# The state's read of x in 32-column weights, four heads in four column groups of the PE array, with its sums from ScalarE's accumulator

## Chip, cores and metric

One core of a Trainium2 chip. The metric is the device time of one execution in microseconds (us), the median of several runs. All runs quoted are fast: the granted TensorE clock was 0.998 to 1.000 of full speed in every one of them. Ratios are the mean time of one kernel's fast runs over that of the other's fast runs of the same rounds, so they are not quite the ratio of the medians quoted beside them.

## The reference

Eight batches, each with 8 heads, 512 tokens of 64 dimensions and 32 states. The tokens read the state, the state reads the tokens, and both results go through a two-dimensional Fourier mix, a norm and an MLP. The part at issue is `sread`.

```python
scores2 = scale * np.matmul(state, x.transpose(0, 1, 3, 2))
scores2 = scores2 - scores2.max(-1, keepdims=True)
a2 = np.exp(scores2)
a2 /= a2.sum(-1, keepdims=True) + 1e-09
sread = np.matmul(a2, x)                       # per head: (32 x 512) @ (512 x 64)
...                                            # Fourier mix, norm
ch = np.maximum(un @ w_ch1, 0.0) @ w_ch2       # the MLP, most of the work
return (u + ch).astype(np.float32)
```

## The kernel before

Two words first. Each matmul leaves two records in the trace: the load of its weight (LDWEIGHTS, engine PEld) and the matmul (engine PE), for which the columns of the other operand, the moving columns, are streamed. PSUM is the memory that the results land in.

`E` holds exp(scores) with tokens on the partitions: four blocks `si` of 128 tokens, two halves `g` of four heads, and 128 columns (4 heads x 32 states). `turn_scores` turns it over into `ET`, with states on the partitions. The state's read uses `E` as the weight. A weight has the columns of four heads, so each matmul multiplies every one of the four heads' states with every one of the four heads' x, and only the four blocks on the diagonal are used. A column of ones beside x gives the sums.

```python
def turn_scores(g):
    p = qt("eTp")
    for si, o, rhs in (...):                                     # cut
        nc.tensor.matmul(p[:, o:o + rhs.shape[1]], lhsT=E[:, si, g, :], rhs=rhs, start=True, stop=True)
    nc.scalar.copy(ET[:, g, :], p)

def sread():
    rcs = wk.tile([128, 2], F32, name="rcs", tag="rcs")
    for g in range(2):
        p = qt("srp")                                            # one of three PSUM tiles
        for si in range(4):
            nc.tensor.matmul(p[:, 0:257], lhsT=E[:, si, g, :], rhs=xin[:, si, 257 * g:257 * g + 257],
                             start=(si == 0), stop=(si == 3))
        nc.vector.reciprocal(rcs[:, g:g + 1], p[:, 256 * g:256 * g + 1])
        for hh in range(4):
            ...                                                  # cut: c0, ph of the head
            o = XR[0:32, 0, c0:c0 - 64:-1]
            i = p[ph, 1 - g + 64 * hh:65 - g + 64 * hh]
            if g == 0 and b > 0:
                nc.vector.tensor_scalar(o, in0=i, scalar1=rcs[ph, g:g + 1], scalar2=None, op0=ALU.mult)
            else:
                nc.scalar.activation(o, i, AF.Copy, scale=rcs[ph, g:g + 1])

second = [
    lambda: xread(256, True, "xrp", XR[:, 0, 1:513]),
    sread,
    None,
    lambda: xread(0, False, "xfp", XF[:, 0, 0:512], apart=(b == 0)),
    low if b > 1 else lambda: (low(), fold_early()),             # 32 low rows: two matmuls of 260 columns
    ...
]
```

These steps are woven between the matmuls of the MLP (`ph`, layer 1, and `po`, layer 2), so that TensorE always has something to do.

The softmax here doesn't subtract the row's maximum and nothing guards it: scores larger than these inputs give would overflow.

## Time and profile before

| | before |
|---|---|
| median (range) | 320.87 us (320.67 to 321.31) |
| span of the profiled run | 319.8 us |
| busy: TensorE, VectorE, ScalarE | 304.9, 189.1, 145.8 us |
| state's reads from batch 2 on | 6 x 8 matmuls of 257 columns, 0.885 us of TensorE's stream each |

A TensorE record lasts longer than the matmul holds the stream (a 512-column one is recorded at 379 ns and they follow each other every 216), so the cost of a group of matmuls is read from starts: the start of the next group less its own. The 216 ns for 512 columns and 110 for 257 are 0.416 ns a column, or 2.4 columns a nanosecond, and some 3 ns for each matmul. The prediction below shows the lines.

### The profile page before, as it was taken

The page shows a single profiled execution, that of the slowest core. Times are in us where ns is not written, and L with a number is a line of the kernel's source. Part 1 is how long each engine was busy: PE and PEld are TensorE (multiplying, and loading weights), DVE is VectorE, ACT ScalarE, POOL GpSimd, SP SyncE. Part 2 cuts the span into 40 slices and gives each one's busy share as a digit, 9 for nine tenths or more (in the row PEclk, how much of TensorE's full clock was granted, in tenths as well). Part 3 has the DMA queues.
Part 4 walks back from the last instruction along what each step waited for, and adds up shares of the span by engine and source line. Part 5 has one row for each costly group of instructions (what it writes and reads, how often), then busy time and mean ns, then how long its engine had stood idle before and what let it go on. Part 6 is the DMA issues. An engine that isn't in the chain of part 4 may idle for free.

```text
span 319.8 us, 5768 instructions
## 1 busy us (share of the span) xinstructions
PE 304.9 (95%) x2206; PEld 177.8 (56%) x2206; DVE 189.1 (59%) x451; ACT 145.8 (46%) x283; POOL 73.1 (23%) x167
## 2 busy tenths in 40 slices
PE   5979998899999999999999999999999999999995
PEld 5858986454554555555645554555454544455444
DVE  8797576669586693781816865595658583101112
ACT  6798763844544444334343434434443332343200
POOL 8658693500240020300320024001200030000000
PEclk9999999999999999999999999999999999999999
DMA  7998997425855925239243443630352025302064
GB/s 141 203 197 162 207 188 132 80 65 118 177 87 117 197 68 124 64 82 194 69 96 66 84 116 82 133 84 33 81 86 66 33 47 120 82 35 66 35 137 126
DMA packets 111532, 34.22 MB, mean 107 GB/s; under 512 B 102928, under 2 KB 107280, under 8 KB 111504
## 3 DMA queue, kind: packets, MB, share of 16 engines
q1 hardware_dynamic: 100784, 28.08, 41.8%
q0 software_dynamic: 4224, 4.19, 8.1%
q10 hardware_dynamic: 6496, 1.57, 2.4%
q8 instruction: 17, 0.28, 0.4%
q14 instruction: 11, 0.09, 0.1%
HBM read 22.43 MB, written 14.02 MB: 114 GB/s over the span
## 4 chain that ended last, share of the span: by engine, by line
PE 79%; DVE 14%; ACT 3%; issue 2%; POOL 1%; DMA 1%; DVEq 0%; POOLq 0%; ACTq 0%
PE po L719 31%; PE ph L653 29%; PE gp L533 3%; PE warm L739 2%; PE ph L663 2%; PE srp L429 2%; DVE U L503 2%; DVE st L314 1%; PE yp L499 1%; DVE XR L419 1%; DVE ot L684 1%; PE yp L498 1%; PE xrp L410 1%; DVE XQ L466 1%; PE xfp L410 1%
## 5 line engine op out<-in xcount | busy, mean ns | idle before, releaser
L719 PE MATMUL po<-w,hT 128*128 128x512 bf16 x496 | 125.0, 379 | 0.0
L653 PE MATMUL ph<-unT,w 128*128 128x512 bf16 x448 | 114.5, 379 | 0.9 <-DVE ot L684 0.8
L655 ACT ACTIVATE hT<-ph 128x512 bf16<-128x512 f32 x112 | 66.8, 597 | 102.2 <-PE ph L653 102.0
L653 PEld LDWEIGHTS <-w 128*128 128x128 bf16 x576 | 51.3, 98 | 48.9 <-issue 1.7
L719 PEld LDWEIGHTS <-hT 128*128 128x128 bf16 x496 | 47.5, 98 | 44.9
L684 DVE SCALAR_TENSOR_TENSOR ot<-po,rstd,U 128x512 f32<-128x512 f32 (+1 forms) x33 | 24.2, 733 | 55.8 <-PE po L719 51.5
L543 POOL COPY GL<-G 128x128 bf16<-128x128 bf16 x8 | 2.4, 299 | 120.6 <-ACT G L541 120.6
L503 DVE TENSOR_TENSOR U<-yp,XR 128x512 f32<-128x512 f32 x16 | 10.9, 683 | 22.4 <-PE yp L499 22.4
L314 DVE BATCH_NORM_STATS2 st<-U 128x6 f32<-128x512 f32 x32 | 21.8, 681 | 0.1
L319 POOL TENSOR_TENSOR rstd<-rstd,mhalf 128x1 f32<-128x1 f32 x34 | 20.3, 596 | 2.7
L440 ACT ACTIVATE XR<-srp,rcs 32x64 bf16<-32x64 f32 x36 | 11.1, 309 | 21.0 <-DVE rcs L431 20.4
L318 POOL TENSOR_TENSOR rstd<-mv,epst 128x1 f32<-128x1 f32 x34 | 6.5, 191 | 60.5 <-DVE mv L316 60.5
L739 PE MATMUL warm<-ident 128*128 128x128 bf16 x182 | 15.4, 241 | 3.5 <-POOL ident masks.py:199 3.4
L541 ACT CAST G<-gp 128x288 bf16<-128x288 f32 x31 | 12.2, 396 | 12.7 <-PE gp L533 6.7
L663 PE MATMUL ph<-unT,w 128*128 128x128 bf16 x256 | 16.2, 219 | 0.2 <-ACT unT L577 0.2
L739 PEld LDWEIGHTS <-ident 128*128 128x128 bf16 x182 | 13.6, 110 | 4.2 <-POOL ident masks.py:199 3.4
L663 PEld LDWEIGHTS <-w 128*128 128x128 bf16 x256 | 15.2, 98 | 0.6 <-issue 0.3
L533 PEld LDWEIGHTS <-XQ 128*128 128x128 bf16 x96 | 8.6, 98 | 9.3 <-DVE XQ L466 3.8
L136 POOL CAST xin<-xs 128x2048 bf16<-128x2048 f32 x7 | 13.2, 1891 | 0.0
L567 DVE TENSOR_SCALAR ub<-U,mv 128x512 bf16<-128x512 f32 x24 | 12.3, 512 | 1.0 <-DVE mv L316 0.2
L410 PEld LDWEIGHTS <-ET 128*128 128x128 bf16 x80 | 7.2, 98 | 9.2 <-DVE XL L419 0.8
L419 DVE TENSOR_TENSOR XR<-xrp,rs 128x512 bf16<-128x512 f32 x16 | 11.1, 695 | 0.9 <-POOL XR L276 0.3
(181 smaller groups left out, 368.0 us busy)
## 6 DMA issues: line engine op xcount, KB each, us to landing
xs<-in_x_dram SPq DMA_DIRECT2D x30, 256.0 KB, 4.6
w<-in_moe_w_ch_dram POOLq DMA_DIRECT2D x8, 512.0 KB, 10.8
out_dram<-ot SPq DMA_DIRECT2D x15, 256.0 KB, 2.7
r_dram<-ot SPq DMA_DIRECT2D x14, 256.0 KB, 2.2
out_dram<-r_dram SPq DMA_DIRECT2D x14, 256.0 KB, 3.7
xs<-in_x_dram ACTq DMA_DIRECT2D x2, 256.0 KB, 3.5
l_dram<-ot SPq DMA_DIRECT2D x2, 256.0 KB
r_dram<-ot ACTq DMA_DIRECT2D x2, 256.0 KB
```

Of the source, the lines that this page charges most:

```text
L314: nc.vector.bn_stats(st6, u)
L319: nc.gpsimd.tensor_tensor(rstd, rstd, mhalf, op=ALU.pow)
L410: nc.tensor.matmul(ph[:, 0:260], lhsT=ET[:, g, c0:c0 + 128], rhs=rhs, start=True, stop=True)
L419: nc.vector.tensor_tensor(ov, in0=p[ps, :, 0:256].rearrange("p g (h d) -> p g h d", d=D), in1=rs[ps].unsqueeze(3).to_broadcast([n, 2, 4, D ...
L503: nc.vector.tensor_add(u.rearrange("p (k r) -> p k r", r=2), p.rearrange("p (r k) -> p k r", r=2)[:, 0:u.shape[1] // 2, :], x.rearrange("p ...
L533: nc.tensor.matmul(p[:, 0:NM], lhsT=XQ[:, j, c, :], rhs=tab[c], start=(c == 0), stop=(c == 2 and j != 2))
L653: nc.tensor.matmul(ph[:, o:o + n], lhsT=w1[:, c, f * 128:(f + 1) * 128], rhs=un_of[key][:, c, :], start=(c == 0), stop=(c == DC - 1))
L655: nc.scalar.activation(hT[:, per * i:per * i + per, :].rearrange("p a b -> p (a b)"), ph, AF.Relu, scale=-1.0 if key in flipped else 1.0)
L663: nc.tensor.matmul(ph[:, o:o + 128], lhsT=w1[:, c, f * 128:(f + 1) * 128], rhs=un_of[key][:, c, 128 * r:128 * r + 128], start=(c == 0), st ...
L684: nc.vector.scalar_tensor_tensor(ot[:, cols], in0=po_of[i][:, 0:cols.stop - cols.start], scalar=rstd, in1=u[:, cols], op0=ALU.mult, op1=AL ...
L719: nc.tensor.matmul(po_of[i], lhsT=h_of[key][:, f, i * 128:(i + 1) * 128], rhs=w2[:, f, :], start=(f == 0), stop=(f == FC - 1))
L739: nc.tensor.matmul(t[:, 0:128], lhsT=ident, rhs=ident, start=(i == 0), stop=(i == n - 1))
```

## The change

The intent is to stop computing what is thrown away. Each head gets its own 32-column weight and its own 64 columns of x, and writes its own 32 partitions of one PSUM tile. A weight of 32 columns that writes 32 partitions occupies one quarter of the array's columns (a column group), so that four heads may work side by side. The column of ones falls out of the matmul; the sums come instead from the copy that evacuates `ET`, as ScalarE adds up each row as it copies.

```diff
+        sums = wk.tile([128, 2], F32, name="sums", tag="sums")
...
-            nc.scalar.copy(ET[:, g, :], p)
+            nc.scalar.activation(ET[:, g, :], p, AF.Copy, accum_out=sums[:, g:g + 1])
...
+        def sread_by_head():
+            p = qt("srp")
+            for g in range(2):
+                for si in range(4):
+                    for hh in range(4):
+                        c0 = 1 + 256 * g + 64 * hh
+                        nc.tensor.matmul(p[32 * hh:32 * hh + 32, 64 * g:64 * g + 64], lhsT=E[:, si, g, 32 * hh:32 * hh + 32],
+                                         rhs=xin[:, si, c0:c0 + 64], start=(si == 0), stop=(si == 3))
+            rcs = wk.tile([128, 2], F32, name="rcs", tag="rcs")
+            nc.vector.reciprocal(rcs, sums)
+            o = XR[0:32, 0, 512:0:-1].rearrange("p (g h d) -> p h g d", g=2, d=D)
+            for hh in range(4):
+                ph = slice(32 * hh, 32 * hh + 32)
+                nc.vector.tensor_tensor(o[:, hh], in0=p[ph, 0:128].rearrange("p (g d) -> p g d", g=2),
+                                        in1=rcs[ph].unsqueeze(2).to_broadcast([32, 2, D]), op=ALU.mult)
...
-            sread,
+            sread if b < 2 else sread_by_head,
```

## The prediction

> **What bounds the kernel now.** I began with the busy shares and the chain of waits on the page.
>
> ```profile
> PE 304.9 (95%) x2206; PEld 177.8 (56%) x2206; DVE 189.1 (59%) x451; ACT 145.8 (46%) x283; POOL 73.1 (23%) x167
> ...
> PE 79%; DVE 14%; ACT 3%; issue 2%; POOL 1%; DMA 1%; DVEq 0%; POOLq 0%; ACTq 0%
> ```
>
> TensorE is busy for 95% of the 319.8 us span, and no other engine is above 59%. A busy matmul record counts its pipeline too, so I next read TensorE's timeline, where the start of the next group gives the cost in the stream. This is the stretch around the state's read of the last batch (L429):
>
> ```profile
> 234.27 0.38 PE L410 MATMUL xrp<-stb,ET 128*128 128x260 bf16 x2
> 234.49 1.03 PE L719 MATMUL po<-w,hT 128*128 128x512 bf16 x4
> 235.35 1.05 PE L429 MATMUL srp<-xin,E 128*128 128x257 bf16 x8
> 236.24 1.02 PE L719 MATMUL po<-w,hT 128*128 128x512 bf16 x4
> ```
>
> The starts touch: four 512-column matmuls fill 0.86 us (216 ns each), eight 257-column ones fill 236.24 - 235.35 = 0.89 us (110 ns each). The table of busy time by stretch says the same: TensorE 34.00 us busy of 34.00 in each of 108 to 142, 181 to 215 and 215 to 249 us. From 63 us, where batch 2 reads its state, until 260 us, the table of waits charges TensorE with 2.0 us in all: 0.7 for one transposition, 0.6 for the fold (VectorE, L466), 0.5 for an output and 0.2 for an activation. So in the part that the change touches a nanosecond on TensorE is a nanosecond of the end, and a nanosecond on VectorE or ScalarE is nearly free.
>
> **What the Trainium skill says.** Three places bear on it.
> - "TensorEngine Tiling (Array Packing)", Key Properties and Instruction Overhead: tiles of the array work independently, but "Changing tiling mode (not just tile) drains the TensorE", and a matmul of 1 column costs as much as one of 60. Its restrictions add that column tiling turns the fast weight load off. Every group in this trace is marked 128*128, so the trace shows neither the gain nor the drain.
> - "TensorE: Matmul & The Clock Gate", Part 3 (Measured speedup vs the span model): a pack of tiles takes one matmul's duration and about 4 ns for each further tile; three column tiles at 512 columns gave 2.38 times. That is for 512 columns, where ours have 64. Nothing here confirms it yet.
> - The same page, Part 2 (Back-to-back issue gap): N / 2.4 + 2.5 ns when warm. This gives 109.6 ns for 257 columns and 29.2 for 64. The trace agrees, with 110 above and with the scores' group, which has 64 columns and a new weight for each matmul:
>
> ```profile
> 116.77 0.40 PE L385 MATMUL esp<-sT,xT 128*128 128x64 bf16 x8
> 117.00 0.81 PE L719 MATMUL po<-w,hT 128*128 128x512 bf16 x3
> ```
>
> Eight pairs of weight load and matmul take 0.23 us, 29 ns a pair. I found no price for ScalarE's accumulator output on a page.
>
> **The change part by part.** Only batches 2 to 7 change, so each figure is times 6.
>
> *TensorE, removed:* per batch 8 matmuls of 257 columns, 0.885 us on the path (0.89, 0.88 and 0.88 in the timeline of three batches), 5.3 us in all. That is the ceiling of a gain by this route: 1.7%, even if the new read cost nothing.
>
> *TensorE, added:* per batch 32 pairs, each a 32-column weight and 64 moving columns. The array's useful work falls from 8 x 257 = 2056 column slots to a quarter of 32 x 64 = 2048, if four column groups run at once; if they run one after another it stays the same. The number of instructions goes up fourfold, since the order of the changed program on TensorE has 288 rows more (6 batches x 24 more loads and 24 more matmuls). At the 29 ns of the scores' pairs: 32 x 29 = 0.93 us, which is 0.05 more per batch, +0.3 us in all. I take this as the base, since a 64-column matmul is near the floor already (about 28 ns for 32 columns: the three matmuls of L397 that begin with the identity take 0.14 us, two of which are 128 columns at 56).
>
> *TensorE, the mode:* each read goes from whole-array tiles to column tiles and back, two switches. If the array drains, the cost is what lies between a matmul's streaming and its end. The scores' record lasts 193 ns with 27 ns of streaming (64 / 2.4), so about 166 ns. Two at full price are 0.33 us per batch, 2.0 in all. Part of it can lie beside weight loads already under way, so I count half, +1.0 us.
>
> *ScalarE:* the rows concerned, from the groups by form:
>
> ```profile
> L440 ACT ACTIVATE XR<-srp,rcs 32x64 bf16<-32x64 f32 x36 | 11.1, 309 | 21.0 <-DVE rcs L431 20.4
> L438 DVE TENSOR_SCALAR XR<-srp,rcs 32x64 bf16<-32x64 f32 x28 | 7.9, 281 | 0.6
> L398 ACT CAST ET<-eTp 128x512 bf16<-128x512 f32 x12 | 7.0, 584 | 1.6 <-PE eTp L397 1.5
> L431 DVE RECIPROCAL rcs<-srp 128x1 f32<-128x1 f32 x16 | 2.7, 166 | 3.2 <-PE srp L429 2.9
> ```
>
> Removed are 4 x 309 = 1.24 us per batch, 7.4 us in all, and the wait for the second reciprocal that held ScalarE's queue (20.4 us at 8 places, 2.5 or so each). Added is the sum of each of the 12 casts of L398. If it is read by a separate small instruction of some 200 ns (my guess), that is 0.4 us per batch. ScalarE gets about 5 us lighter, all beside TensorE. On the path it can give back only the single 0.2 us that TensorE waited for an activation.
>
> *VectorE:* removed are 2 x 166 + 4 x 281 = 1456 ns; added are one reciprocal (168) and four products of 32 x 128 read from PSUM. From the products of 256 columns (425 ns, L413) and of 512 (690, L419) the slope is 1.04 ns a column, so 128 columns take about 425 - 133 = 292 ns. Sum: 168 + 4 x 292 = 1336. So VectorE gets 0.1 us lighter per batch. In batch 2 TensorE waits 0.6 us for VectorE's fold, so about 0.1 of it may come back there.
>
> *Buffers:* one PSUM tile of the pool of three in place of two, and it is free as soon as VectorE's products end, not after ScalarE's four late copies (2.7 us after its last matmul's start in the last batch). TensorE shows no wait for that pool in the changed stretch, so this is worth nothing.
>
> Sum: +0.3 + 1.0 - 0.2 = **+1.1 us**, from 320.87 to about **321.9 us**.
>
> **The rivals.**
> - *The column groups overlap as the skill's span model has it.* Then eight rounds of four take 8 x (29 + 3 x 4) = 0.33 us per batch (estimate from that page), 0.56 less than now: -3.3 us; with half the drains -2.3, so about 318.5 us. For it speaks that consecutive matmuls go to different groups and all share one PSUM tile in different quadrants. Against it: each of the 32 matmuls has its own weight load in front, and the floor on a short matmul may be one of issue, which tiles do not lift. I give it 3 in 10.
> - *Loads and matmuls stop overlapping.* Without the fast weight load, or because a column tile's load must wait for the matmul before it, a pair may cost the load and the matmul in turn, 29 + 29 = 58 ns: 32 x 58 = 1.86 us, and with both drains 2.19, which is 1.3 per batch more than now: +7.8 us, about 328.7 us. For it speaks that the trace has no load narrower than the array, so the overlap seen on L385 is not proved for these. I give it 2 in 10, the full price less often.
> - *A wait elsewhere gives more than the sum.* If the ScalarE queue, blocked behind the second reciprocal for 2.6 us per batch, were holding up the relu tiles, freeing it would shorten the chain by several us. The timeline speaks against it: TensorE's starts touch right after each state read. I count it at zero.
>
> **Range and chances.** The three ways give 318.5, 321.9 and 328.7. The quick one sets the low end with some freedom, **317.6**; the slow one at about half its price sets the high end, **326.5**. A gain over 2% needs -6.4 us, more than the whole read costs now (5.3), so **0.02**. A loss over 2% needs +1.07 us per batch, thus a read of 1.95 us, 61 ns a pair with no drain or 51 with both: the slow rival at nearly its full price, **0.11**. The rest, **0.87**, is within 2%.
>
> **What would show it.** In the timeline of the changed kernel, the start of the group after the state's read less the read's start should be 0.93 to 1.26 us, in place of 0.885; 0.35 to 0.5 would mean that the groups overlap, and above 1.8 that loads and matmuls alternate. The start of the first 32-column matmul should lag by up to 0.17 us after the 216 ns slot of the matmul before it, and so should the first matmul after the read, if there is a drain. ScalarE's busy time should fall by about 5 us and its wait on L431 go, VectorE's by about 0.7 us, and TensorE should still show no wait for either from 78 to 260 us. The prediction is wrong if the read's slot is outside 0.5 to 1.8 us, or if the slot is as said and the end still moves by over 3 us, which would mean that a wait elsewhere, or the accumulator's cost, was on the path.

## The result

| | before | after |
|---|---|---|
| median, same chip (4 runs each) | 321.09 us | 318.71 us |
| ratio of the fast runs | | 0.9931, 95% interval 0.9914 to 0.9948 |
| span of the profiled run | 319.8 us | 317.1 us |
| busy: TensorE, VectorE, ScalarE | 304.9, 189.1, 145.8 us | 300.2, 188.1, 139.7 us |
| one state's read in TensorE's stream, batches 2 to 7 | 0.885 us | 0.453 us |

The class is "same" (within 2%), but the gain of 0.7% is clear of noise. Two later repeats of the changed kernel gave 0.9926 and 0.9909. Lines below carry the changed kernel's numbers, 18 higher for code behind the new function: L719 became L737 and L653 became L671.

The page's busy shares and chain of the changed kernel, the answer to the first fence of the prediction:

```profile
PE 300.2 (95%) x2317; PEld 174.7 (55%) x2350; DVE 188.1 (59%) x445; ACT 139.7 (44%) x271; POOL 73.1 (23%) x167
...
PE 79%; DVE 13%; ACT 2%; issue 2%; POOL 1%; DMA 1%; DVEq 0%; POOLq 0%; ACTq 0%
```

TensorE is as much the bound as before. It has some 2350 matmuls in place of 2206 (33 records are missing from the trace; the loads, complete at 2350, show it).

The state's read of batch 7 in the timeline of the changed kernel, loads included (start, duration, engine, line, what, and in brackets the idle time before it):

```profile
232.27 1.03 PE L737 MATMUL po<-w,hT 128*128 128x512 bf16 x4
...
233.23 0.30 PEld L450 LDWEIGHTS <-E 128*32 128x32 bf16 x32 [0.42 <-issue]
233.23 0.43 PE L450 MATMUL srp<-xin,E 128*32 128x64 bf16 x32
...
233.58 0.55 PEld L737 LDWEIGHTS <-hT 128*128 128x128 bf16 x4
...
233.81 0.81 PE L737 MATMUL po<-w,hT 128*128 128x512 bf16 x3 [0.16 <-issue]
```

The last group has lost a record: it has four loads from 233.58 on but only three matmuls. So the "idle 0.16" in front of it is not idle. The repeat of the changed kernel has the same place in batch 5 with every record:

```profile
167.10 1.03 PE L737 MATMUL po<-w,hT 128*128 128x512 bf16 x4
168.06 0.43 PE L450 MATMUL srp<-xin,E 128*32 128x64 bf16 x32
168.42 1.04 PE L737 MATMUL po<-w,hT 128*128 128x512 bf16 x4
```

The read has three parts. In front: 168.06 - 167.10 = 0.96 us, 0.09 more than the 0.86 of four 512-column matmuls. The matmuls: the record of 0.43 us less the 0.193 us that one of them lasts is 0.236 us from the first start to the last. Behind: 0.36 - 0.236 = 0.124 us from the last start to the next group. The sum is 0.453 us. The starts themselves, in ns from the read's first matmul (batch 4 of the changed kernel, taken from the trace's records), show what happened:

```
0 3 7 10 | 38 42 45 49 | 74 78 81 85 | 103 107 110 114 | 132 137 139 143 | 162 166 168 172 | 193 197 200 207 | 222 227 229 237
```

Four matmuls start within 10 to 15 ns, then nothing until the next four, 29 to 31 ns after the start of the ones before (38 and 36 for the first two rounds), which is about what 64 columns take to stream (29 ns). That is how four column groups at work at once would look; the run with one group, below, tests it.

The other engines, from the groups by form of the changed kernel (busy us, mean ns, idle before and its releaser):

```profile
L399 ACT ACTIVATE ET<-eTp 128x512 bf16<-128x512 f32 x12 | 7.1, 596 | 1.6 <-PE eTp L398 1.5
L457 DVE TENSOR_TENSOR XR<-srp,rcs 32x128 bf16<-32x128 f32 x24 | 6.9, 287 | 1.3 <-PE srp L450 0.8
L441 ACT ACTIVATE XR<-srp,rcs 32x64 bf16<-32x64 f32 x12 | 3.7, 309 | 2.4 <-DVE rcs L432 2.3
...
L399 ACT ACTIVATION_READ_ACCUMULATOR ET<-eTp 128x1 f32 x12 | 2.4, 202 | 0.0
...
L453 DVE RECIPROCAL rcs<-sums 128x2 f32<-128x2 f32 x6 | 0.9, 154 | 0.0
```

The accumulator is read by an instruction of its own, 202 ns. ScalarE's wait for the reciprocal fell from 20.4 us to 2.3 (what is left is batches 0 and 1). TensorE's waits of the changed kernel between 63 and 260 us:

```profile
PE tp L594 <- ACT ub L583: 0.7, 1, 0.7
PE po L737 <- issue: 0.6, 4, 0.2
PE gp L551 <- DVE XQ L484: 0.6, 1, 0.6
PE ph L671 <- DVE ot L702: 0.4, 1, 0.4
PE xfp L411 <- DVE XL L420: 0.2, 1, 0.2
```

The 0.6 of "issue" is the lost records again, four times 0.16. The rest is 1.9 us where it was 2.0: the 0.2 that the kernel before waited for an activation (L655) went, and 0.2 for VectorE (L420) came. So the sum is 6 x (0.885 - 0.453) = 2.6 us, and the spans differ by 2.7.

### The profile page after: what moved, and what is told of

Its sections match the earlier page's. It is cut to its first block, busy times and chain, and to the rows that moved or that the text cites. A ratio compares the mean times of both kernels' runs of the same rounds, so it can differ in the third digit from the quotient of the medians.

```text
span 317.1 us, 6003 instructions
## 1 busy us (share of the span) xinstructions
PE 300.2 (95%) x2317; PEld 174.7 (55%) x2350; DVE 188.1 (59%) x445; ACT 139.7 (44%) x271; POOL 73.1 (23%) x167
## 4 chain that ended last, share of the span: by engine, by line
PE 79%; DVE 13%; ACT 2%; issue 2%; POOL 1%; DMA 1%; DVEq 0%; POOLq 0%; ACTq 0%
PE po L737 32%; PE ph L671 30%; PE gp L551 3%; PE warm L757 2%; PE ph L681 2%; DVE U L521 2%; DVE st L314 1%; PE yp L517 1%; PE xfp L411 1%; PE xrp L411 1%; PE yp L516 1%; DVE XQ L484 1%; DVE XE L473 1%; DVE XR L420 1%; DMA out_dram<-ot 1%
## 5 line engine op out<-in xcount | busy, mean ns | idle before, releaser
L737 PE MATMUL po<-w,hT 128*128 128x512 bf16 x477 | 122.2, 379 | 1.3 <-issue 0.6
L673 ACT ACTIVATE hT<-ph 128x512 bf16<-128x512 f32 x112 | 66.9, 597 | 124.3 <-PE ph L671 121.7
L671 PE MATMUL ph<-unT,w 128*128 128x512 bf16 x435 | 113.6, 379 | 1.5 <-DVE ot L702 0.7
L671 PEld LDWEIGHTS <-w 128*128 128x128 bf16 x576 | 51.2, 98 | 48.6 <-issue 1.3
L737 PEld LDWEIGHTS <-hT 128*128 128x128 bf16 x496 | 47.1, 98 | 45.0
L420 DVE TENSOR_TENSOR XR<-xrp,rs 128x512 bf16<-128x512 f32 x16 | 11.1, 695 | 0.9 <-POOL XR L276 0.3
L683 ACT ACTIVATE hT<-ph 128x512 bf16<-128x512 f32 x16 | 9.3, 597 | 4.9 <-PE ph L681 4.9
```

The costliest lines, as they stand in the source:

```text
L420: nc.vector.tensor_tensor(ov, in0=p[ps, :, 0:256].rearrange("p g (h d) -> p g h d", d=D), in1=rs[ps].unsqueeze(3).to_broadcast([n, 2, 4, D ...
L671: nc.tensor.matmul(ph[:, o:o + n], lhsT=w1[:, c, f * 128:(f + 1) * 128], rhs=un_of[key][:, c, :], start=(c == 0), stop=(c == DC - 1))
L673: nc.scalar.activation(hT[:, per * i:per * i + per, :].rearrange("p a b -> p (a b)"), ph, AF.Relu, scale=-1.0 if key in flipped else 1.0)
L737: nc.tensor.matmul(po_of[i], lhsT=h_of[key][:, f, i * 128:(i + 1) * 128], rhs=w2[:, f, :], start=(f == 0), stop=(f == FC - 1))
```

## The experiments

In all of them the results were correct. Executions of one kernel on one chip differ by up to 2.7 us here (the runs of the kernel before went from 320.77 to 323.47 on chip 15), so the slot of the read in the trace, which repeats within 0.01 us, says more than the median. The slot is the sum of three parts: "in front" (the start of the first matmul less the end of the slot of the one before), "starts" (first to last start) and "behind" (last start to the next group's). The expected column is 6 x (slot - 0.885); for the split read it is 5 times that and once the changed kernel's, since in batch 2 the two halves fell together. The "step" column is a check on the slot: the time in the trace from the start of batch 6's read to the start of batch 7's, less the 33.267 us of the kernel before.

| kernel | in front, starts, behind (ns) | slot us | step, ns | expected against before, us | median less before's | ratio, 95% interval |
|---|---|---|---|---|---|---|
| before | 0, 772, 113 | 0.885 | 0 | | | |
| changed, repeated | 93, 236, 124 | 0.453 | -422 | -2.6 | -2.05 | 0.9926 (0.9897 to 0.9954) |
| four in a row of one group | 93, 270, 124 | 0.487 | -385 | -2.4 | -1.15 | 0.9956 (0.9926 to 0.9986) |
| each read twice | 93, 492, 131 | 0.716 | -156 | -1.0 | -0.48 | 0.9984 (0.9956 to 1.0011) |
| two visits | 2 x (93, 114, 125) | 0.664 | -198 | -1.5 | -0.55 | 0.9976 (0.9949 to 1.0003) |
| two groups of 64 | 93, 425, 152 | 0.670 | -204 | -1.3 | -1.17 | 0.9955 (0.9931 to 0.9979) |
| halves of 32 columns | 93, 479, 117 | 0.689 | -183 | -1.2 | +0.35 | 0.9984 (0.9954 to 1.0014) |
| eight in a row | 93, 640, 125 | 0.858 | -14 | -0.2 | +0.12 | 1.0010 (0.9980 to 1.0040) |
| one column group | 93, 951, 124 | 1.168 | +295 | +1.7 | +2.06 | 1.0061 (1.0035 to 1.0087) |
| sums and products only | 0, 771, 109 | 0.880 | -3 | 0.0 | +0.44 | 1.0022 (0.9988 to 1.0056) |
| matmuls only | 93, 236, 125 | 0.454 | -422 | -2.6 | -1.63 | 0.9944 (0.9917 to 0.9971) |

The step agrees with the slot in every run, but for 12 ns or so that each visit costs more: the first two matmuls after it start 226 ns apart in place of 216. So the medians' scatter is not the read's. Much of it lies before the change: in the traces the read of batch 2 starts anywhere between 65.6 and 68.2 us. The +0.35 of the halves, whose step is a gain, is such a case (68.1 us, against 66.4 in the kernel before).

### Which part of the change carries the gain

The changed kernel again, as the mark:

> The changed kernel once more, as the mark for its neighbours on this chip: about 318.7 us, 2.4 us under the kernel before. All theories expect the state's read to hold TensorE for 0.36 us from its first matmul to the next group's, plus about 0.1 us in front.

It came out at 319.06 us, with the slot as expected. Next, everything but the new matmuls:

```diff
-                for si in range(4):
-                    for hh in range(4):
-                        c0 = 1 + 256 * g + 64 * hh
-                        nc.tensor.matmul(p[32 * hh:32 * hh + 32, 64 * g:64 * g + 64], ...)
+                for si in range(4):
+                    nc.tensor.matmul(p[:, 256 * g:256 * g + 256], lhsT=E[:, si, g, :],
+                                     rhs=xin[:, si, 1 + 256 * g:257 + 256 * g], start=(si == 0), stop=(si == 3))
 ...                                                     # cut: the products read their head's columns
```

> The sums from ScalarE's accumulator and the products on VectorE as in the change, but the matmuls as before: 8 a batch, whole array, now 256 columns each. My account (everything of this lies beside TensorE): as the kernel before, 321 us, at most 0.3 us less. Rival (the freed ScalarE queue or the buffer that comes free sooner gives a good part of the 2.4 us): 319.5 or less.

Measured: 321.44 us, ratio 1.0022 with an interval that spans 1. The freed ScalarE queue and the PSUM tile that comes free sooner give no gain that can be measured here: the interval leaves room for 0.4 us, and from batch 2's read to batch 7's the trace is 0.16 us shorter. The counterpart keeps the new matmuls and the accumulator, and gives half the products back to ScalarE:

```diff
-            nc.vector.reciprocal(rcs, sums)
-            ...                                        # four products on VectorE
+            for g in range(2):
+                nc.vector.reciprocal(rcs[:, g:g + 1], sums[:, g:g + 1])
+                for hh in range(4):
+                    ...
+                    if g == 0:
+                        nc.vector.tensor_scalar(o, in0=i, scalar1=rcs[ph, g:g + 1], scalar2=None, op0=ALU.mult)
+                    else:
+                        nc.scalar.activation(o, i, AF.Copy, scale=rcs[ph, g:g + 1])
```

> The 32 matmuls in column groups and the sums from the accumulator, but the products as before: half on VectorE, half on ScalarE, with two reciprocals. My account: as the changed kernel, 318.7 us within 0.3. Rival (ScalarE's relief counts): clearly above it, 319.5 or more.

Measured: 319.37 us, ratio 0.9944 (0.9917 to 0.9971), and the same slot as in the changed kernel. It is 0.3 us from the repeat of the changed kernel, which ran in another call, and by the medians that may be noise. The trace shows a wait of TensorE, though, that no trace of the changed kernel has (`--waits`, 63 to 260 us):

```profile
PE ph L675 <- ACT hT L677: 0.6, 1, 0.6
```

It stands in batch 2: ScalarE's queue holds four products that wait 3.4 us for a reciprocal, and the activation of the MLP behind them comes late. The kernel before has the same wait with 0.2 us; the shorter read lengthens it, so that batch 2 gains nothing (27.56 us from its read to the next, 27.51 before, 27.02 in the changed kernel). So the gain is the matmuls', and the accumulator makes them possible; but taking the products off ScalarE is worth about 0.5 us in that one batch, since without it the wait eats the saving there. That is one trace, and no run repeats it.

### Is it the four groups, or the narrow weights?

The first attempt only changed the order of the same 32 matmuls:

```diff
-                for si in range(4):
-                    for hh in range(4):
+                for hh in range(4):
+                    for si in range(4):
```

> The same 32 matmuls, but all four of one head before the next head, so that mostly neighbours in the queue go to the same column group. Theory A (the gain comes from four groups working at once): neighbours can't overlap, a pair costs some 29 ns, the read 0.93 us and the slot about 1.05 instead of 0.36, so +0.65 to 0.7 us a batch, about +4 us over the changed kernel (322.7). Theory B (the gain comes from the narrow weights and short records alone, whatever the order): 318.7, no change. If loads of a group also wait for its matmul, 58 ns a pair: about +9.5 us (328).

Measured: 319.96 us, and a slot of 0.487 us instead of some 1.05. Theory A in the form I gave it fell: neighbours in the queue need not go to different groups. Taken alone this even spoke for theory B. The test that tells them apart makes it impossible for anything to overlap, by sending all 32 to one column group:

```diff
-                for si in range(4):
-                    for hh in range(4):
-                        nc.tensor.matmul(p[32 * hh:32 * hh + 32, 64 * g:64 * g + 64], ...)
+                for hh in range(4):
+                    for si in range(4):
+                        o0 = 64 * (4 * g + hh)
+                        nc.tensor.matmul(p[0:32, o0:o0 + 64], ...)
...
-                nc.vector.tensor_tensor(o[:, hh], in0=p[ph, 0:128]...
+                nc.vector.tensor_tensor(o[:, hh], in0=p[0:32].rearrange("p (g h d) -> p h g d", g=2, d=D)[:, hh],
```

> The same 32 matmuls of 32-column weights and 64 moving columns, but all write partitions 0 to 31 of the tile, side by side in its 512 columns: one column group does it all, and nothing can run beside it. Theory A (four groups working at once are the gain): 29 ns a pair as the prediction's base had it, 32 x 29 = 0.93 us for the read, slot about 1.1 us in place of 0.45, so +0.65 us a batch and +4 us over the changed kernel: about 322.7 to 323. Theory B, left over from the order run (the 12 to 14 ns between the starts of neighbours in one group are their real pace): 0.45 us, +1.2 us, about 320. If a load there waits for the matmul before it, 58 ns a pair: about +10 us.

Measured: 323.24 us, slower than the kernel before (1.0061, interval above 1). Its timeline in batch 3:

```profile
94.51 1.03 PE L738 MATMUL po<-w,hT 128*128 128x512 bf16 x4
95.47 1.14 PE L451 MATMUL srp<-xin,E 128*32 128x64 bf16 x32
```

The same 32 weights and columns take 1.14 - 0.19 = 0.95 us from first start to last, 951 / 31 = 31 ns a pair, where four groups take 0.236: four times as long. So the gain is the four groups at once. Narrow weights alone, one after another, are a loss. The load is not in the way: a pair costs what its 64 columns cost.

With 29 to 31 ns for each pair of one group, the order run has a lesson. If matmuls started strictly in program order, four in a row of one group would need 3 x 29 = 87 ns before the next group could begin, 8 x 87 = 0.70 us for the read; it took 0.27. So matmuls of another group must have gone ahead of ones that waited for their own. How far does that go?

```diff
-            for g in range(2):
-                for si in range(4):
-                    for hh in range(4):
+            for hh in range(4):
+                for g in range(2):
+                    for si in range(4):
```

> All eight matmuls of a column group before the next group's. If TensorE can hold back a group's matmuls and start those of other groups in the meantime (as four in a row suggest, where the read lost only 0.03 us), there is a limit to how far it looks. No limit within 32: about 0.3 us from first start to last start, as with four in a row. If at most four wait for a group: each run of eight stalls the queue for some four slots of 29 ns, 0.24 + 3 x 0.1, so about 0.55 us. If really in order: 4 x 8 x 29 = 0.93 us.

Measured: 0.64 us from first to last start and 321.3 us, as slow as the kernel before. Strict order would give 4 x 7 x 29 = 0.81. That is nearest to the middle expectation: other groups go ahead, but only a few places. The starts of batch 3, in ns, say how many:

```
eight in a row    0 38 74 103 132 138 161 176 193 212 222 241 270 276 ...
one column group  0 39 74 104 133     162     194     223
```

The first group's eight starts stand where they stand in the run with one column group. Other starts come between them, the first 6 ns after the fifth of the eight, and the same step returns at 270 to 276 and at 410 to 416. So the next group went ahead of three waiting matmuls and not of more; the last group then needs its 223 ns, and 416 + 223 = 639 is the read. The records don't say which group a matmul belonged to, so this is read from the agreement of the starts. No run tests the depth in another way.

### What a pair costs, and what sets it

```diff
-            for g in range(2):
+            for g in (0, 1, 0, 1):
```

> The 32 matmuls of each read are done a second time straight after the first, into the same place, with no further change of tiling. It prices the matmuls without the switch. Theory A (8 ns a pair, eight rounds of 30 ns): +0.24 us a batch, +1.4 us over the changed kernel (320.1). If the 0.36 us were mostly switching, +0.5 us or less; if 29 ns a pair really held, +5.6.

Measured: 64 matmuls in 0.492 us, so the second 32 cost 0.256 us, and the time rose by 1.6 us over the repeat of the changed kernel (320.63 against 319.06). That is 6 x 0.26. Then wider weights in two groups:

```diff
-                    for hh in range(4):
-                        nc.tensor.matmul(p[32 * hh:32 * hh + 32, 64 * g:64 * g + 64], ...)
+                    for hp in range(2):
+                        c0 = 1 + 256 * g + 128 * hp
+                        nc.tensor.matmul(p[64 * hp:64 * hp + 64, 128 * g:128 * g + 128],
+                                         lhsT=E[:, si, g, 64 * hp:64 * hp + 64],
+                                         rhs=xin[:, si, c0:c0 + 128], start=(si == 0), stop=(si == 3))
 ...                                                     # cut: the products read their head's columns
```

> 16 matmuls a batch with 64-column weights (two heads) and 128 moving columns, in two column groups. Theory A (time is columns over 2.4 GHz divided by the number of groups, plus the switch): 8 rounds of 56 ns, 0.45 us, plus 0.19: 0.64 a read, 0.19 to 0.21 over the changed kernel's 0.45, so +1.2 us over it (319.9). If issue set the pace (7.6 ns a pair), 16 pairs would take 0.12 us and the time would fall below the changed kernel's; if the load is slower for 64 columns, more than +1.2.

Measured: the starts come in pairs, some 56 ns from pair to pair, and the read takes 0.425 us from first to last start: the slot is 0.670, as worked out (0.64 to 0.66). The median is 319.83. And the same columns in twice as many matmuls:

```diff
+                for half in range(2):
                     for si in range(4):
                         for hh in range(4):
-                            rhs=xin[:, si, c0:c0 + 64]
+                            c0 = 1 + 256 * g + 64 * hh + 32 * half     # and 32 columns of p
+                            rhs=xin[:, si, c0:c0 + 32]
```

> The same read in 64 matmuls of 32 moving columns each, every one with its own load. It asks what sets the 7.6 ns a pair. If streaming does (32 columns are 13 ns, over four groups 3.3): 64 x 3.3 = 0.21 us, no change, 318.7. If a group can start a matmul only every 28 ns or so: 16 rounds of 28 = 0.45 us, +0.21 a batch, +1.3 us (320). If issue does (7.6 ns a pair whatever the columns): 64 x 7.6 = 0.49, +0.25 a batch, +1.5 us. The last two differ in the pair's pace within the trace.

Measured: 0.479 us for 64 pairs, in two regimes. The first 32 pairs go in rounds of four every 25 ns; the last 32 come singly, 8.4 ns apart. So a group starts a matmul at most every 25 ns, and from about the 33rd pair on a pair of load and matmul costs about 8 ns. That this is the pace of issue, once what was queued ahead is used up, is my reading; no run shows it apart. The changed kernel needs 236 / 31 = 7.6 ns a pair, close to both limits (29 / 4 = 7.3 and 8), and smaller pieces gained nothing here.

### The price of changing the tiling

```diff
-            sread if b < 2 else sread_by_head,
-            None,
+            sread if b < 2 else sread_first,            # heads 0 to 3
+            None if b < 2 else sread_by_head,           # heads 4 to 7, and the products
```

> The read is split: heads 0 to 3 where it was, heads 4 to 7 one step later, between other matmuls. The same 32 matmuls, but four changes of tiling a batch in place of two. Theory A (each way in and out costs about 0.1 us, 0.19 for both): +0.19 us a batch, +1.1 us over the changed kernel (319.8). Rival (the lag is only the first load's latency hidden elsewhere, and costs the end nothing): no change.

The timeline of the two visits in batch 5:

```profile
166.84 1.03 PE L746 MATMUL po<-w,hT 128*128 128x512 bf16 x4
167.80 0.31 PE L455 MATMUL srp<-xin,E 128*32 128x64 bf16 x16
168.03 1.04 PE L746 MATMUL po<-w,hT 128*128 128x512 bf16 x4
169.00 0.30 PE L455 MATMUL srp<-xin,E 128*32 128x64 bf16 x16
169.24 1.03 PE L680 MATMUL ph<-unT,w 128*128 128x512 bf16 x4
```

Both visits pay the 0.09 us in front (167.80 - 166.84 and 169.00 - 168.03 are 0.96 and 0.97 in place of 0.86). Behind, each pays 125 ns where the last matmul's own turn would be 29. So the way in and the way out cost 93 + 95 = 0.19 us a visit, and the split read is 0.21 us longer (0.22 by the step). The median rose by 1.5 us over the repeat; the slots account for 1.05 of it, the rest is within the noise.

What the lag is made of shows in the loads. In the kernel before, the first load of a read starts 214 ns ahead of its matmul, beside the 512-column matmul in front; in the changed kernel it starts 2 ns ahead, and the first load after the visit 4 ns ahead. So no load went ahead across a change of tiling. Whether the array also has to empty first is not told apart from this.

### A version that beats both

If the way in and out costs 0.19 us a visit, other narrow work should ride in the same visit. The read of the 32 low rows is such: it uses 32 of its 128 weight columns. Four pieces (half `g` of the heads, half of the 260 columns) fit into four column groups. The products then read a partition group and write the rows' own.

```diff
+        def sread_and_low():
+            sread_by_head()
+            p = qt("xlp")
+            for g in range(2):
+                for half in range(2):
+                    q = 32 * (2 * g + half)
+                    nc.tensor.matmul(p[q:q + 32, 0:132], lhsT=ET[:, g, 256:288], rhs=sb[:, g, 132 * half:132 * half + 132],
+                                     start=True, stop=True)
+            ...                                         # one reciprocal of the sums, four products on VectorE
...
-            sread if b < 2 else sread_by_head,
+            sread if b < 2 else sread_and_low,
...
-            low if b > 1 else lambda: (low(), fold_early()),
+            None if b > 1 else lambda: (low(), fold_early()),
```

> The changed kernel as the mark for the next run on this chip: about 2.2 us under the kernel before, 318.9 us. The 0.22 us of the low rows' read (two matmuls of 260 columns) stay where they are.

> From batch 2 on the read of the 32 low rows, two whole-array matmuls of 260 columns (0.22 us, one step of its own), becomes four matmuls of 32-column weights and 132 columns in four column groups, in the same visit as the state's read, so no further change of tiling. If the account holds: one round of 132 / 2.4 + 2.5 = 58 ns in place of 220, so the visit grows from 0.45 to about 0.51 us and 0.16 us a batch is saved, 1.0 us in all: 317.9. VectorE gets two products of 687 ns worth as four of 290 and is 0.5 us busier a batch, which should stay beside TensorE. If VectorE's extra work early in the reads delays the next read's tile, TensorE shows a wait there and the gain is smaller or gone.

(The text says two products of 687 ns; it is one a batch, with a reciprocal of 201.) Measured: 318.80 us for the changed kernel (0.9909, 0.9885 to 0.9933) and 317.47 us for this one (0.9869, 0.9842 to 0.9896), 1.3 us less. The timeline in batch 5:

```profile
165.85 1.03 PE L755 MATMUL po<-w,hT 128*128 128x512 bf16 x4
166.81 0.43 PE L450 MATMUL srp<-xin,E 128*32 128x64 bf16 x32
167.06 0.23 PE L466 MATMUL xlp<-stb,ET 128*32 128x132 bf16 x4
167.23 1.04 PE L755 MATMUL po<-w,hT 128*128 128x512 bf16 x4
```

The visit is 0.09 + 0.42 = 0.51 us as worked out, and the step of 0.22 us for the low rows is gone: 0.16 us a batch, 1.0 us in all. VectorE is busy for 190.5 us (187.3 in the changed kernel's run), and TensorE's waits did not grow.

## Why the prediction was right, and where it was wrong

Its range held (318.71 us in 317.6 to 326.5), and so did the class. Its central number, +1.1 us, had the wrong sign, and the first rival was what happened: it said 318.5. So the range held through a rival that was given 3 in 10, and not through the mechanism that the prediction favoured. Its high end is also not what it says: half of the slow rival's +7.8 us would be 324.8, and 326.5 is 72% of it.

- **What bounds the kernel** held. A nanosecond on TensorE was one of the end: 6 x 0.432 = 2.6 us of slots gave 2.7 us of span and 2.4 us of median. A nanosecond on the others was nearly free: the run with only their part of the change gave 1.0022, interval across 1. The 0.2 us of waiting for an activation did go, as the prediction allowed, and a wait of 0.2 us for VectorE took its place. It had not seen that a shorter read would lengthen that wait if the products stayed on ScalarE (0.6 us in the run with the matmuls only).
- **TensorE, added** is the step that failed: "At the 29 ns of the scores' pairs: 32 x 29 = 0.93 us". The pair price itself was right, but for one column group, where the run with a single group measured 0.95 us. Four groups do it in 0.236 us from first to last start. With that in place of 0.93 us the prediction's own sum would have had a gain, as its quick rival did. The base took a floor seen in whole-array matmuls (28 ns for 32 columns) for one of the queue. It is one of each group: neighbours in different groups start 3 to 4 ns apart.
- **The mode** held. I counted 0.17 us a read, half of two drains of 166 ns; the runs show 93 + 95 = 0.19 us. The half was a guess that came out. The cost is not small: without it a read would have saved 0.62 us in place of 0.43.
- **The quick rival** put the read at 0.33 us plus 0.17; measured 0.236 plus the last matmul's 29 ns, plus 0.19. It had used 12 ns of stagger on each of the eight rounds. But the stagger lies within the time that a round streams, so that rounds follow every 29 to 31 ns after the first two.
- **The slow rival** (58 ns a pair) did not occur in any run: even in one group a pair cost 31 ns.
- **ScalarE** fell by 6.1 us where I said about 5. Removed are 24 x 309 = 7.4 us; added are 12 x 202 = 2.4, but each read of the accumulator starts about 0.1 us before the copy's record ends, so that it adds less busy time. The guess of 200 ns was right.
- **VectorE**: 154 + 4 x 287 = 1302 ns a batch where I had 1336.
- **Its own test**: it said that it would be wrong if the slot were outside 0.5 to 1.8 us. As it defines the slot, from the read's start to the next group's, it is 0.36 us, outside (and 0.453 with the lag in front). By its own measure the mechanism it favoured was wrong, and its line that 0.35 to 0.5 would mean overlapping groups read the result correctly.

## What to carry to other kernels

Where a weight has several independent blocks and only the diagonal of the product is used, give each block its own column group: with 32-column weights four of them stream at once, here 0.236 us in place of 0.95 in one group and 0.885 with the whole array. Reckon with about 0.19 us for going into the tiling and out of it again, so gather narrow work into one visit, and put the groups next to each other in the queue. On a kernel that one engine bounds, price that engine's slots first: the accumulator, the products and the freed queue of this change gave nothing measurable by themselves. Then look for the waits that a shorter slot uncovers: with half the products left on ScalarE, one wait of 0.6 us took batch 2's share of the gain.

## What the Trainium skill lacked or had wrong

- "TensorE: Matmul & The Clock Gate", Part 3, says that matmuls start and end in strict program order. Runs of four matmuls of one column group took 0.27 us, where strict order needs 0.70 at the 29 ns of a group. So matmuls of different column groups pass each other here, as far as the starts tell by three places: runs of eight took 0.64 us, strict order 0.81.
- The same page, Part 1 ("Wait — 56ns, not 53.3ns?"), says that start-to-start never drops below about 25 ns however few the columns. Across column groups the starts are 3 to 4 ns apart, which fits the 4 ns for each further tile that the prediction took from Part 3; the 25 ns hold for one group (rounds of 25 ns with 32 columns). A second pace is on no page: about 8 ns for a pair of load and matmul in a long run of them (8.4 with 32 columns; 256 / 32 = 8.0 in the doubled read).
- The same page, Part 3, says in its list of what overlaps that a load overlaps with matmuls in flight only when the row group differs, though just above it also names a background weight buffer. Here all use all rows, and in one column group a pair costs 31 ns, about its 64 columns alone, so the load is hidden.
- "TensorEngine Tiling (Array Packing)", Key Properties, says that a change of tiling drains the engine, without a price: 93 ns in front and 95 behind, and the same for 64-column tiles (93, and 152 less the 56 of a round is 96). The runs show that no load goes ahead across the change; they don't show a drain apart from that.
- The same page, Restrictions, says that column tiling turns the fast weight load off. No run here shows a cost of it: loads of 32 and 64 columns stayed beside 64 and 128 moving columns.
- No page has the price of ScalarE's accumulator output: a separate instruction of 202 ns after each activation.
